# A Fourier transform over 3136 points, factored 56 by 56 where it was 64 by 49

## The chip, the cores and the metric

The kernel is one program on one core of a Trainium2 chip. The metric is device microseconds of that core from start to end of one execution; lower is better. The kernel before was timed three times: 1010.18, 1008.93 and 1010.29 us, median 1010.18 us.

## The reference

The input `x` is 8 sequences of 3136 rows of 256 numbers. The kernel computes, in single precision,

```python
X = np.fft.fft(x, axis=1)            # over the 3136 rows
X = np.fft.fft(X, axis=2)            # over the 256 columns
x = X.real.astype(np.float32)
mu = np.mean(x, axis=-1, keepdims=True)
var = np.mean((x - mu) ** 2, axis=-1, keepdims=True)
xn = (x - mu) / np.sqrt(var + 1e-06) * g_ln
ch = np.maximum(xn @ w_ch1, 0.0) @ w_ch2     # 256 -> 1024 -> 256
return x + ch
```

`g_ln`, `w_ch1` and `w_ch2` are inputs.

## The kernel before, in words

**Two halves per sequence.** The input is real and only the real part is wanted, so of the 3136 frequencies of a sequence (a batch, b = 0 to 7) only half have to be computed; a column of the kernel stands for frequency k and gives the output rows k and N-k. There are 1567 such columns in a batch and they are worked off in chunks of 256 (49 chunks, c).

**Step 1** of the transform runs over u, the 64 values with n = 49u + v. The 25 values of v that have to be kept (the others follow by symmetry) are laid out on two halves of the 128 partitions as 14 slots (`NS`), two slots to a unit (`NU` = 7, index i). For batches 1 to 7 each unit goes through a chain of small steps: `load_x` (SP's DMA queue), `fold_zw` and `fold_eo` (POOL), `fold_hi` (ACT, a rounding to the short float32 form, fp32r), `fold_lo` (POOL, the rest), `step1` (PE, three products for high and low pieces, L262, into PSUM bank `y`), a copy by ACT (L265), and `store1` to a scratch in DRAM. For batch 0 the products are full float32 (L255, L257), the folds are DVE's, and the stores go through ACT's and POOL's DMA queues in turn. `ends` and `step1_ends` treat columns 0 and 128 of the rows. A unit has two slots of 2 x 128 columns, so one product of L262 has 512 columns.

**Step 2.** `relayout` reads the scratch back with the rows turned round, as `s2` on `KP` = 112 partitions and 16 groups of 98 columns (the first has 99). `step2(m)` is one pair of groups: for each group and each of two halves h a full float32 product (L309), which PE runs as two instructions with a weight load each, so 8 instructions for a pair and 8 pairs in a batch, 64 pairs in all. For the first pair one more small product is added (L313). ACT copies the result into the chunk (`ck`, `ckh`: L332, L330) and DVE forms the low pieces (`ckl`, L334).

**The rest of the work** is the network: `moe1_a` (6 products of 256 columns, L354, and ACT and DVE work on them), `moe1_b` (L368, L369) and `moe2` (12 products of 256 columns, L404) for each of 8 parts of a chunk, and `residual` (the real output itself and its variance, 8 instructions per chunk, L428).

**Order.** The order of PE, ACT, DVE and POOL is written out by hand, and each engine works its list off in that order. A prologue (from L685) brings in batch 0, converts the weights of the network and fills PE's waiting time with products on zeros (`warm_up`, L682). Then a loop over steps s (from L825), one part of one chunk each: `moe1_b(s-1)`, `moe1_a(s)`, what `late[s]` holds, `moe2(s-3)`, what `after[s]` holds. `add` and `add_late` fill those lists. `step2(m)` stands three steps before the chunk that it begins, at the same step as the chunk's `residual`; where two pairs begin in one chunk, the second uses bank `y`. `steps1` gives the step of each unit of step 1: in 20 places over batches 2 to 7 that is the very step that holds step 2 and the residual, behind these on PE.

Of the kernel before, what the change touches and what calls it, by code (L numbers as in the profile page):

```python
# [29 lines left out]
NV = 25  # L30
# [9 lines left out]
NS = 14  # L40
ROWS = NB * N
NU = NS // 2
KP = 8 * NS


def unit_k(unit):
    if unit == 0:
        return np.concatenate([[0, N // 2], 64 * np.arange(1, 25), 32 + 64 * np.arange(24)])
    return unit + 64 * np.arange(49)


def runs():

    units = [unit for g in range(16) for unit in (g, 16 + g)]
    return [r for unit in units for r in (((49, unit),) if unit else ((24, 64), (24, 32)))]


def group_bounds():
    return [0] + [99 + 98 * g for g in range(16)]


def tables():
    u = np.arange(64)[:, None]
    t1 = np.zeros((64, 64))
    t1[:, :33] = np.cos(2 * np.pi * u * np.arange(33) / 64)
    t1[:, 33:] = np.sin(2 * np.pi * u * np.arange(1, 32) / 64)
    th = np.zeros((64, 64))
    th[:, 1:32] = -np.sin(2 * np.pi * u * np.arange(1, 32) / 64)
    th[:, 33:] = np.cos(2 * np.pi * u * np.arange(1, 32) / 64)
    tu = np.zeros((128, 388))  # L70
    for par in range(2):
        s = slice(64 * par, 64 * par + 64)
        tu[s, s] = t1
        tu[s, 128 + 64 * par:192 + 64 * par] = -t1
        tu[s, 256 + 64 * par:320 + 64 * par] = th
        tu[s, 384 + 2 * par] = 1.0
        tu[s, 385 + 2 * par] = np.cos(np.pi * np.arange(64))
    vs = ((0, np.arange(1, 15)), (1, np.append(np.arange(15, NV), 0)))
    tab = np.zeros((2, 2, 2, NS, 2, HALF))
    tz = np.zeros((4, NS, 50))  # L80
    t = 0
    for g in range(16):
        for q in range(2):
            k = unit_k(g + 16 * q)
            n = len(k)
            for par, v in vs:
# [3 lines left out]
                for comp in range(2):  # L90
                    rows = tab[par, comp, q, :m]
                    if n == 50:
                        half = np.flatnonzero(k % 64 == 32 * comp)
# [5 lines left out]
    tab = tab.transpose(3, 0, 1, 2, 4, 5).reshape(112, 2, HALF)  # L99
    tz = np.concatenate([tz.reshape(4 * NS, 50), np.zeros((KP - 4 * NS, 50))])  # L100
# [18 lines left out]
def input_rows():  # L119

    v = np.full((2, NS), -1)
    v[0] = np.arange(1, 15)
    v[1, :11] = np.append(np.arange(15, NV), 0)
    n = np.where(v[:, None] < 0, N, 49 * np.arange(64)[None, :, None] + v[:, None])
    minus = np.where(v[:, None] <= 0, N, N - n)
    both = np.stack([n, minus], 2).reshape(128, 2, NU, 2)
    return both.transpose(2, 0, 1, 3).reshape(NU, 128, 4)  # L130


def output_rows():

    k = np.concatenate([k0 + 64 * np.arange(n) for n, k0 in runs()])
# [11 lines left out]
def tile_kernel(ctx: ExitStack, tc: tile.TileContext, x, g_ln, w1, w2, tu, tab, tz, ty, tw, out):  # L147
# [14 lines left out]
    t1_hi = weights.tile([128, 128], F32R, name="t1_hi")  # L162
    t1_lo = weights.tile([128, 128], F32R, name="t1_lo")
    tu_s = const.tile([128, 388], F32, name="tu_s")
    tab_s = const.tile([KP, 2, HALF], F32, name="tab_s")
    tz_s = const.tile([KP, 50], F32, name="tz_s")
    tw_all = const.tile([128, 640], F32, name="tw_all")
# [4 lines left out]
    xs = const.tile([128, NU, 4, D], F32, name="xs")  # L172
    zmu = const.tile([KP, 2, 128], F32, name="zmu")
    masked = const.tile([128, KP], F32, name="masked")
# [4 lines left out]
    def load_x(b, i):  # L179
        in_order(nc.sync.dma_start(xs[:, i], x[b, i]))  # L180
# [3 lines left out]
    def ends(b, p0=0, p1=NS, eng=nc.gpsimd):  # L184

        if p0 == 0:
            e0c[b] = work.tile([128, NS, 2], F32, tag="e0c", name=f"e0c{b}")
        e = e0c[b]
        xp = xs[:, p0 // 2:p1 // 2, :, 0:129:128]
        eng.tensor_tensor(out=e[:, p0:p1].rearrange("p (i a) c -> p i a c", a=2), in0=xp[:, :, 0:2],  # L190
                          in1=xp[:, :, 2:4], op=ALU.add)
        if p1 < NS:
            return
        eng.tensor_tensor(out=masked[:, :4 * NS].rearrange("p (c s) -> p c s", c=4),
                          in0=e[:, None, :, 0].to_broadcast([128, 4, NS]),
                          in1=tu_s[:, 384:388, None].to_broadcast([128, 4, NS]), op=ALU.mult)

    def fold_zw(b, i, eng):

        if i > 3 and b == 0:  # L200
# [3 lines left out]
        z, w = (t[:, 256 * h:256 * h + 256].rearrange("p (s d) -> p s d", s=2) for h in range(2))  # L204
# [5 lines left out]
    def fold_eo(b, i):  # L210
        z, w = zw.pop((b, i))
        f = work.tile([128, 2, 2, 128], F32, tag="fold", name=f"f{b}_{i}")
        nc.gpsimd.tensor_tensor(out=f[:, :, 0], in0=z, in1=w, op=ALU.add)
        nc.gpsimd.tensor_tensor(out=f[:, :, 1], in0=z, in1=w, op=ALU.subtract)
        pieces[b, i] = [f]

    def fold_hi(b, i):
        hi = moving.tile([128, 2, 2, 128], F32R, tag="f_hi", name=f"fh{b}_{i}", bufs=2)
# [3 lines left out]
    def fold_lo(b, i):  # L222
        f, hi = pieces[b, i]
        lo = moving.tile([128, 2, 2, 128], F32R, tag="f_lo", name=f"fl{b}_{i}", bufs=2)
# [633 lines left out]
```

## Time and profile before

| | |
|---|---|
| times of three runs | 1010.18, 1008.93, 1010.29 us |
| profiled execution, first to last instruction | 1008.9 us |
| PE busy | 99% of the span, 8289 products |
| DVE, ACT, POOL busy | 81%, 53%, 25% |
| granted TensorE clock | 1.0 throughout |
| chain of work that ended last | PE 93%, DVE 4%, ACT 2%, DMA 1% |
| moved by DMA | 92.10 MB, mean 91 GB/s |

The span is 1.3 us under the median of the runs. Times inside it count from its start. A product is pipelined: its duration in the profile (some 280 ns) is longer than its share of PE's time, which is the distance from its start to the start of the next. The chain of work that ended last gives these distances: a row of it is a run of instructions of one line, with the time from one to the next summed up.

### The profile page before, as it was taken

What the parts mean: (1) busy time and instruction counts of PE and PEld (TensorE: products, weight loads), DVE (VectorE), ACT (ScalarE), POOL (GpSimd) and SP (SyncE); (2) the same over time, 40 slices, a digit from 0 to 9 for tenths busy, and PEclk for the clock granted to TensorE, in tenths of its full rate; (3) what the DMA queues carried; (4) which work ended last, traced back from release to release, by engine and by line L of the source; (5) the groups of instructions that cost most, each with busy time, mean ns of one, the idle gap of its engine ahead of it and who ended that gap; (6) DMA issues with size and microseconds to landing.
All of it is one profiled execution on the core that took longest, in us unless ns stands there. A gap on an engine that the chain in (4) does not pass through costs nothing.

```text
span 1008.9 us, 21765 instructions
## 1 busy us (share of the span) xinstructions
PE 998.4 (99%) x8289; PEld 976.5 (97%) x8289; DVE 817.2 (81%) x2190; ACT 534.7 (53%) x1416; POOL 248.5 (25%) x278
## 2 busy tenths in 40 slices
PE   9899999999999999999999999999999999999998
PEld 6699999999999999999999999999999999999998
DVE  6688887888778788878887888888788878887887
ACT  3555555555555555555555555554555554554553
POOL 1146533134213232312341224123323200000000
PEclk9999999999999999999999999999999999999999
DMA  9943352214221261121521242211311112100101
GB/s 343 265 164 95 116 168 74 85 53 136 85 93 55 74 177 65 56 85 60 158 84 54 84 130 91 94 54 63 116 43 43 54 55 83 41 24 22 43 22 43
DMA packets 41528, 92.10 MB, mean 91 GB/s; under 512 B 4176, under 2 KB 18704, under 8 KB 40528
## 3 DMA queue, kind: packets, MB, share of 16 engines
q1 hardware_dynamic: 40016, 88.87, 26.8%
q8 instruction: 66, 1.08, 0.5%
q0 software_dynamic: 320, 1.05, 0.3%
q10 hardware_dynamic: 1088, 0.79, 0.2%
q14 instruction: 38, 0.31, 0.1%
HBM read 50.32 MB, written 40.37 MB: 90 GB/s over the span
## 4 chain that ended last, share of the span: by engine, by line
PE 93%; DVE 4%; ACT 2%; DMA 1%; issue 0%; SPq 0%; DVEq 0%; ACTq 0%
PE acc L404 51%; PE ab L354 26%; PE ps L309 6%; PE psy L428 4%; PE ps L262 3%; DVE h_lo L369 1%; PE pw L682 1%; PE ps L255 1%; DMA scratch<-s 1%; PE ps L257 1%; DVE h L360 1%; DVE h L361 1%; ACT h_hi L368 0%; DMA s<-scratch 0%; ACT asb L359 0%
## 5 line engine op out<-in xcount | busy, mean ns | idle before, releaser
L404 PE MATMUL acc<-w_hi,h_lo 128*128 128x256 f32 x1568 | 437.9, 279 | 0.2 <-DVE h_lo L369 0.2
L404 PE MATMUL acc<-w_lo,h_hi 128*128 128x256 f32 x1568 | 437.7, 279 | 0.0
L404 PE MATMUL acc<-w_hi,h_hi 128*128 128x256 f32 x1568 | 437.6, 279 | 0.0
L368 ACT ACTIVATE h_hi<-h 128x512 fp32r<-128x512 f32 x392 | 249.3, 636 | 308.4 <-DVE h L361 308.3
L369 DVE SCALAR_TENSOR_TENSOR h_lo<-h,h_hi 128x512 fp32r<-128x512 f32 x392 | 282.0, 719 | 158.1 <-ACT h_hi L368 157.0
L404 PEld LDWEIGHTS acc<-w_hi,h_lo 128*128 128x128 f32 x1568 | 296.7, 189 | 0.6 <-DVE h_lo L369 0.4
L404 PEld LDWEIGHTS acc<-w_lo,h_hi 128*128 128x128 f32 x1568 | 295.4, 188 | 0.0
L404 PEld LDWEIGHTS acc<-w_hi,h_hi 128*128 128x128 f32 x1568 | 295.1, 188 | 0.0
L354 PE MATMUL ab<-ckl,w_hi 128*128 128x256 f32 x768 | 218.5, 285 | 1.8 <-DVE h L361 1.8
L354 PE MATMUL ab<-ckh,w_lo 128*128 128x256 f32 x768 | 214.9, 280 | 0.5 <-ACT ckh L330 0.3
L354 PE MATMUL ab<-ckh,w_hi 128*128 128x256 f32 x768 | 214.5, 279 | 0.0
L225 POOL TENSOR_TENSOR fl<-f,fh 128x512 fp32r<-128x512 f32 x49 | 64.2, 1309 | 518.6 <-ACT fh L219 512.4
L360 DVE TENSOR_TENSOR h<-asb,ab 128x256 f32<-128x256 f32 x384 | 158.2, 412 | 1.5 <-ACT asb L359 1.5
L361 DVE TENSOR_TENSOR h<-asb,ab 128x256 f32<-128x256 f32 x384 | 158.1, 412 | 0.0
L354 PEld LDWEIGHTS ab<-ckl,w_hi 128*128 128x128 f32 x768 | 145.3, 189 | 5.9 <-ACT w_hi L539 1.5
L354 PEld LDWEIGHTS ab<-ckh,w_lo 128*128 128x128 f32 x768 | 144.7, 188 | 3.1 <-ACT ckh L330 0.5
L354 PEld LDWEIGHTS ab<-ckh,w_hi 128*128 128x128 f32 x768 | 144.6, 188 | 0.0
L359 ACT COPY asb<-ab 128x256 f32<-128x256 f32 x384 | 137.8, 359 | 8.1 <-PE ab L354 6.2
L265 ACT COPY s<-ps 128x508 f32<-128x508 f32 x56 | 32.7, 584 | 64.9 <-PE ps L262 51.0
L309 PE MATMUL ps<-tab_s,s 112*128 112x98 f32 (+1 forms) x512 | 65.6, 273 | 1.5 <-DMA s<-scratch 1.5
L309 PEld LDWEIGHTS ps<-tab_s,s 112*128 112x128 f32 x512 | 61.9, 192 | 2.0 <-issue 2.0
L330 ACT CAST ckh<-ps 128x392 fp32r<-128x392 f32 (+49 forms) x112 | 39.7, 356 | 40.6 <-PE ps L309 40.4
(108 smaller groups left out, 980.5 us busy)
## 6 DMA issues: line engine op xcount, KB each, us to landing
xs<-x SPq DMA_DIRECT2D x56, 512.0 KB, 3.8
out<-o SPq DMA_DIRECT2D x96, 256.0 KB, 2.0
scratch<-s SPq DMA_DIRECT2D x49, 256.0 KB, 2.3
s<-scratch SPq DMA_DIRECT2D x7, 1792.0 KB, 9.8
w1p_all<-w SPq DMA_DIRECT2D x8, 512.0 KB, 8.3
scratch<-s POOLq DMA_DIRECT2D x4, 256.0 KB, 6.3
s<-scratch SPq DMA_DIRECT2D x2, 448.0 KB, 5.3
s<-scratch SPq DMA_DIRECT2D x1, 896.0 KB, 11.2
```

Of the source, the lines that this page charges most:

```text
L225: nc.gpsimd.tensor_tensor(out=lo, in0=f, in1=hi.bitcast(F32), op=ALU.subtract)
L265: nc.scalar.copy(s[:, :, :, :127], ps[:, :, :, :127])
L309: nc.tensor.matmul(ps[:, h, k0 - base:k1 - base], s2[b][:KP, g, 128 * h:128 * h + 128], tab_s[:, h, k0:k1], start=(h == 0 and g == 2 * j), ...
L330: nc.scalar.copy(hi, src)
L354: nc.tensor.matmul(pt, wt[wi][:, j, fs], ch[xi][:, j, :w], start=(n == 0), stop=(n == 2))
L359: nc.scalar.copy(asb[:, :w], pa)
L360: nc.vector.tensor_tensor(out=h[:, :w], in0=asb[:, :w], in1=pb, op=ALU.add)
L361: nc.vector.tensor_tensor(out=h[:, w:], in0=asb[:, :m], in1=pb[:, :m], op=ALU.subtract)
L368: nc.scalar.activation(h_hi, h, AF.Relu)
L369: nc.vector.scalar_tensor_tensor(out=h_lo, in0=h, scalar=0.0, in1=h_hi.bitcast(F32), op0=ALU.max, op1=ALU.subtract)
L404: nc.tensor.matmul(acc[c, i][:, side], hs[xi][:, h0:h0 + 128], ws[wi][:, f], start=(f == 0 and side == 0 and n == 0), stop=(f == 7 and n = ...
L428: nc.tensor.matmul(ps[:, j, :129 + j], ck[:, j], ty_s[:, j, :129 + j], start=(j == 0), stop=True, skip_group_check=True)
```

## The change

The factors become 56 and 56. Step 1 runs over 56 values of u on 112 partitions (`XP`), and 29 values of v have to be kept: 28 fill 14 slots as before, and the value v = 0 gets a fifteenth slot, on the first 56 partitions, with its own load (`x0` into `xz`) and its own short unit (i = `NU` = 7, one slot). Step 2 has 14 groups of 112 columns on 116 partitions, so 7 pairs in a batch, where it was 16 groups of 98 on 112 and 8 pairs. For batches 1 to 7 step 1's three products are made for each slot alone, 256 columns each, six for a full unit and three for the short one. The steps of the units are set anew, none of them at the step of step 2 and the residual. The last unit's store takes three slots. The table `tw_all` is put into one of the buffers of `ck_hi`; `tz_s`, `zmu` and `masked` become smaller. The core of the diff:

```diff
-NS = 14
+R1 = 56
+XP = 2 * R1
+NU = 7
+NS = 2 * NU + 1
+NG = 14
+KP = 8 * 2 * NU + 4
+KZ = 4 * NS
+NM = NG // 2
 def group_bounds():
-    return [0] + [99 + 98 * g for g in range(16)]
+    return [0] + [2 * R1 + 1 + 2 * R1 * g for g in range(NG)]
...
-    xs = const.tile([128, NU, 4, D], F32, name="xs")
+    xs = const.tile([XP, NU, 4, D], F32, name="xs")
+    xz = const.tile([XP, D], F32, name="xz")
...
     def load_x(b, i):
-        in_order(nc.sync.dma_start(xs[:, i], x[b, i]))
+        if i == NU:
+            in_order(nc.sync.dma_start(xz[:R1], x0[b]))
+        else:
+            in_order(nc.sync.dma_start(xs[:, i], x[b, i]))
...
+        eng.tensor_copy(e[:, NS - 1], xz[:, 0:129:128])
...
+    def slots(i):
+
+        return 1 if i == NU else 2
+
+    def fold_eo(b, i, eng=nc.gpsimd):
+        n = slots(i)
+        z, w = zw.pop((b, i)) if n > 1 else (xz[:, None, 1:129], xz[:, None, 255:127:-1])
+        f = work.tile([128, 2, 2, 128], F32, tag="fold", name=f"f{b}_{i}")[:XP, :n]
+        eng.tensor_tensor(out=f[:, :, 0], in0=z, in1=w, op=ALU.add)
+        eng.tensor_tensor(out=f[:, :, 1], in0=z, in1=w, op=ALU.subtract)
...
+        if b == 0 and n == 1:
+            nc.tensor.matmul(ps, tu_p, pieces.pop((b, i))[0], start=True, stop=True)
...
             p = pieces.pop((b, i))
-            for n, (ti, xi) in enumerate(PASSES):
-                nc.tensor.matmul(ps, (t1_hi, t1_lo)[ti], p[xi],
-                                 start=(n == 0), stop=(n == 2))
+            for a in range(n):
+                for j, (ti, xi) in enumerate(PASSES):
+                    nc.tensor.matmul(ps[:, a], (t1_hi, t1_lo)[ti], p[xi][:, a],
+                                     start=(a == 0 and j == 0), stop=(j == 2),
+                                     skip_group_check=True)
...
     def store1(b, i, eng=nc.sync):
-        s = s1[b][:, 2 * i:2 * i + 2]
+        n = 3 if i == NU - 1 else 2
...
-    for m in range(3, 64):
+    for m in range(3, NM * NB):
...
-    steps1 = {1: [17, 20, 23, 26, 28, 31, 34]}
-    for b in range(2, NB):
-        need = 8 * (b * REG // CW) - 3
-        steps1[b] = sorted([need - 46, need - 45] +
-                           [behind(need - d) for d in (56, 40, 32, 24, 16)])
     for b in range(1, NB):
         need = 8 * (b * REG // CW) - 3
-        at = steps1[b]
-        ends_at = need - (58 if b > 1 else 30)
+        behind = (54, 45, 38, 30, 25, 21, 14, 34)
+        at = [need - d for d in behind] if b > 1 else [17, 20, 23, 28, 30, 33, 35, 25]
+        ends_at = need - (55 if b > 1 else 30)
...
-        add(at[-1] + 2, relayout, b)
+        add(max(at) + 2, relayout, b)
...
             load_x(0, 1)
+            load_x(0, NU)
...
             ends(0, 6, 10)
             fold_zw(0, 3, nc.vector)
+            fold_eo(0, NU)
             step1(0, 3)
+            step1(0, NU)
```

## Rows read from the trace of the kernel before

**Rows 1.** The page's first part (busy time and share of the span of each engine, instructions) and the first line of its fourth (the chain that ended last).

```profile
PE 998.4 (99%) x8289; PEld 976.5 (97%) x8289; DVE 817.2 (81%) x2190; ACT 534.7 (53%) x1416; POOL 248.5 (25%) x278
...
PE 93%; DVE 4%; ACT 2%; DMA 1%; issue 0%; SPq 0%; DVEq 0%; ACTq 0%
```

**Rows 2.** Busy time in three stretches of the span; behind the length come busy us and instructions of PE, PEld, DVE, ACT and POOL, then the granted clock, the share of the DMA engines and GB/s.

```profile
8.12:22.14 14.02, 14.02 (x72) 12.29 (x71) 11.54 (x25) 5.50 (x14) 3.60 (x7) 1.00 1.03 411
22.14:34.28 12.14, 10.61 (x33) 4.45 (x32) 8.37 (x15) 6.25 (x12) 1.15 (x2) 1.00 0.77 237
...
64.00:990.00 926.00, 924.79 (x7840) 917.29 (x7840) 756.61 (x2046) 498.50 (x1329) 232.78 (x251) 1.00 0.24 79
```

**Rows 3.** The longest of PE's waits from 64 us to the end: total us, times, longest.

```profile
PE ps L262 <- DVE ckl L334: 1.2, 1, 1.2
```

**Rows 4.** The chain that ended last, from 206 to 234 us: start, us, engine, output, line, instructions.

```profile
206.22 1.41 PE acc L404 x12
207.64 0.71 PE ab L354 x6
...
218.80 0.70 PE ps L262 x3
...
220.19 1.36 PE acc L404 x12
221.55 0.68 PE ab L354 x6
...
231.75 0.87 PE ps L309 x8
232.62 0.92 PE psy L428 x8
```

**Rows 5.** One of the three like groups of L404's products, by shape, from 64 to 990 us: count, busy us, mean ns of one (the pipelined duration), idle before.

```profile
L404 PE MATMUL acc<-w_hi,h_lo 128*128 128x256 f32 x1504 | 419.9, 279 | 0.0
```

**Rows 6.** The chain that ended last, in the first six stretches of 16 to 20 us that begin with step 2 and a residual and hold no step 1 (from 844 us on), one row of each.

```profile
848.66 1.36 PE acc L404 x12
...
867.90 1.36 PE acc L404 x12
...
886.12 1.41 PE acc L404 x12
...
904.87 1.41 PE acc L404 x12
...
924.43 1.36 PE acc L404 x12
...
942.64 1.41 PE acc L404 x12
```

**Rows 7.** The same view where a unit of step 1 stands right behind the residual, the first products of L404 behind it: the first and the last of 20 such places.

```profile
136.01 1.41 PE acc L404 x12
...
827.87 1.41 PE acc L404 x12
```

**Rows 8.** The chain that ended last through the end of step 1 of batch 0.

```profile
21.24 0.43 PE ps L255 x2
...
22.14 0.59 ACT s L265
...
23.02 6.31 DMA scratch<-s
...
29.54 4.61 DMA s<-scratch
```

**Rows 9.** PE's instructions in order of time: the first of unit 4's products in batch 0, and the last filler with the start of step 2 (start, us, in brackets the idle time before and its releaser).

```profile
15.47 0.59 PE L255 MATMUL ps<-zw,tu_s 128*128 128x256 f32 x2
...
29.35 3.40 PE L682 MATMUL pw<-warm_h 128*128 128x512 bf16 x15
34.28 0.66 PE L309 MATMUL ps<-tab_s,s 112*128 112x99 f32 x4 [1.54 <-DMA s<-scratch]
```

**Rows 10.** POOL's instructions in order of time, 14 to 16 us.

```profile
14.46 1.62 POOL L269 DMA_DIRECT2D scratch<-s  x2 [3.94 <-ACT s L243]
16.11 0.23 POOL L190 TENSOR_TENSOR e0c<-xs 128x8 f32<-128x8 f32 x1
```

**Rows 11.** Groups of POOL's instructions by shape: count, busy us, mean ns of one, idle before.

```profile
L214 POOL TENSOR_TENSOR f<-zw 128x256 f32<-128x256 f32 x49 | 50.2, 1024 | 0.0
L213 POOL TENSOR_TENSOR f<-zw 128x256 f32<-128x256 f32 x49 | 39.2, 799 | 3.1
```

**Rows 12.** DMA queues: POOL's (q0) in the microsecond from 26 us, SP's (q1) in the one from 27 us, POOL's in the one from 28 us (packets, MB, share of 16 engines), and the issues of the scratch stores on POOL's queue (KB each, median us to landing).

```profile
q0 software_dynamic: 58, 0.19, 47.3%
...
q1 hardware_dynamic: 176, 0.33, 86.9%
...
q0 software_dynamic: 5, 0.02, 5.4%
...
scratch<-s POOLq DMA_DIRECT2D x4, 256.0 KB, 6.3
```

**Rows 13.** The relayout of batch 1 in the order of SP's queue and its landing (KB each, median us), and PE's first product that reads it.

```profile
130.20 0.33 SPq L276 DMA_DIRECT2D s<-scratch  x1
...
s<-scratch SPq DMA_DIRECT2D x7, 1792.0 KB, 9.8
...
152.10 0.58 PE L309 MATMUL ps<-tab_s,s 112*128 112x99 f32 x4
```

More of the change, by code (lines that the diff above doesn't have):

```diff
@@ L39 @@
 HW = 576
-NS = 14
+R1 = 56
[6 more added lines that the diff above has]
+NM = NG // 2
 ROWS = NB * N
-NU = NS // 2
-KP = 8 * NS
 def unit_k(unit):
     if unit == 0:
-        return np.concatenate([[0, N // 2], 64 * np.arange(1, 25), 32 + 64 * np.arange(24)])
-    return unit + 64 * np.arange(49)
+        return np.concatenate([[0, N // 2], R1 * np.arange(1, 28), 28 + R1 * np.arange(28)])
+    return unit + R1 * np.arange(R1)
 def runs():
-    units = [unit for g in range(16) for unit in (g, 16 + g)]
-    return [r for unit in units for r in (((49, unit),) if unit else ((24, 64), (24, 32)))]
+    units = [unit for g in range(NG) for unit in (g, NG + g)]
+    return [r for unit in units for r in (((R1, unit),) if unit else ((27, R1), (28, 28)))]
@@ new lines, in slot_rows @@
+def slot_rows():
+    v = np.full((2, NS), -1)
+    v[0] = np.append(np.arange(1, 15), 0)
+    v[1, :2 * NU] = np.arange(15, 29)
+    return v
+def tables():
+    u = np.arange(R1)[:, None]
+    k1 = np.arange(1, 28)
+    t1 = np.zeros((R1, R1))
+    t1[:, :28] = np.cos(2 * np.pi * u * np.arange(28) / R1)
+    t1[:, 28:29] = np.cos(np.pi * u)
+    t1[:, 29:] = np.sin(2 * np.pi * u * k1 / R1)
+    th = np.zeros((R1, R1))
+    th[:, 1:28] = -np.sin(2 * np.pi * u * k1 / R1)
+    th[:, 29:] = np.cos(2 * np.pi * u * k1 / R1)
+    tu = np.zeros((XP, 3 * XP + 4))
+    for par in range(2):
+        r = slice(R1 * par, R1 * par + R1)
+        for m, t in enumerate((t1, -t1, th)):
+            tu[r, XP * m + R1 * par:XP * m + R1 * par + R1] = t
+        tu[r, 3 * XP + 2 * par] = 1.0
+        tu[r, 3 * XP + 1 + 2 * par] = np.cos(np.pi * np.arange(R1))
@@ L79, in tables @@
     tab = np.zeros((2, 2, 2, NS, 2, HALF))
[L80 removed]
+    tz = np.zeros((4, NS, R1 + 1))
     t = 0
[L82 removed]
+    for g in range(NG):
         for q in range(2):
[L84 removed]
+            k = unit_k(g + NG * q)
             n = len(k)
[L86 removed]
+            for par, v in enumerate(slot_rows()):
+                v = v[v >= 0]
                 al = 2 * np.pi * ((v[:, None] * k) % N) / N
@@ L119, in input_rows @@
 def input_rows():
[L124 to L130, printed above, removed]
+    v = slot_rows()[:, None, :2 * NU]
+    n = R1 * np.arange(R1)[None, :, None] + v
+    minus = np.where(v == 28, N, N - n)
+    both = np.stack([n, minus], 2).reshape(XP, 2, NU, 2)
+    return both.transpose(2, 0, 1, 3).reshape(NU, XP, 4)
 def output_rows():
-    k = np.concatenate([k0 + 64 * np.arange(n) for n, k0 in runs()])
+    k = np.concatenate([k0 + R1 * np.arange(n) for n, k0 in runs()])
     plus = (N * np.arange(NB)[:, None] + k).ravel()
@@ L208, in fold_zw @@
         eng.tensor_tensor(out=w, in0=a[:, :, 255:127:-1], in1=c[:, :, 1:129], op=ALU.add)
[L210 to L214, printed above, removed]
+    def slots(i):
[6 more added lines that the diff above has]
+        eng.tensor_tensor(out=f[:, :, 1], in0=z, in1=w, op=ALU.subtract)
         pieces[b, i] = [f]
     def fold_hi(b, i):
-        hi = moving.tile([128, 2, 2, 128], F32R, tag="f_hi", name=f"fh{b}_{i}", bufs=2)
+        hi = moving.tile([128, 2, 2, 128], F32R, tag="f_hi", name=f"fh{b}_{i}", bufs=2)[:XP, :slots(i)]
         nc.scalar.copy(hi, pieces[b, i][0])
@@ L247, in step1 @@
     def step1(b, i):
         alloc1(b)
+        n = slots(i)
         ps = psum.tile([128, 2, 2, 128], F32, tag="y" if b else f"acc{i % 2}", name=f"ps1_{b}_{i}",
-                       bufs=1 if b else 2)
-        if b == 0:
+                       bufs=1 if b else 2)[:XP, :n]
+        if b == 0 and n == 1:
+            nc.tensor.matmul(ps, tu_p, pieces.pop((b, i))[0], start=True, stop=True)
+        elif b == 0:
             z, w = zw.pop((b, i))
-            for h in range(2):
+            for h, t in ((0, tu_p), (1, tu_n)):
@@ L765, in tile_kernel @@
             nc.sync.dma_start(tab_s[:, :, gb[8]:], tab[:, :, gb[8]:])
-            for i in range(NU):
+            for i in range(NU + 1):
                 load_x(1, i)
```

123 lines of the change are left out of this document (55 added, 68 removed).

## The prediction

> **What bounds the kernel now.** I read the busy shares first, then the chain that ended last, then the waits of PE, then the stretches of the span. PE is busy 99% of the span and makes 93% of the chain [rows 1], and from 64 us to the end nothing but 1.2 us of one wait stands out [rows 2, 3]. So between 64 and 990 us time is the sum of the distances between PE's products, and an instruction less there is time less; DVE with 757 of 926 us and POOL with 233 have room [rows 2]. Before 34 us it is another matter: step 1 of batch 0 keeps PE busy without a gap from 8.12 to 22.14 us, its last store and the relayout follow one upon the other, and step 2 starts on the landing [rows 2, 8, 9]. What is added to that path delays everything behind it.
>
> **Step 2.** Each pair is 8 instructions; 64 pairs become 56, and none of the three pairs in the prologue goes. So 64 instructions leave the loop. Eight take 0.87 us there, 0.109 us each [rows 4]. The new ones have 112 columns, not 98, a width that no row shows; the nearest are the residual's, 129 and 130 columns, full float32 too: eight take 0.92 us, 0.115 each [rows 4]. Below, 98 columns' price is the bound, since nothing makes a wider product cheaper. With 0.109 the gain is 64 x 0.109 = 7.0 us; with 0.115 it is 512 x 0.109 - 448 x 0.115 = 4.3 us. I take 7.0: 31 columns more cost 6 ns, part of which is the change back to other products, and 14 columns more should cost under 3. A check from another side: the float32 products of 256 columns take 0.215 us (two in 0.43) [rows 8], 0.84 ns a column, so 112 columns need 94 ns for themselves, still under the 109 that 98 columns take; something that doesn't go with the columns sets the distance.
>
> The Trainium skill speaks against that in "TensorE: Matmul & The Clock Gate", section "Back-to-back issue gap": it gives an isolated gap of N / 2.4 + 2.5 ns for N columns, so that time goes with columns, of which step 2 keeps as many as it had; by it the 64 instructions would return little more than 2.5 ns each, 0.2 us. The trace disagrees, 98 and 129 columns lying within 6 ns [rows 4]. What it would make of the time is the second rival.
>
> **Step 1, batches 1 to 7.** A unit is three products of 512 columns, 0.70 us [rows 4]. Six of 256 columns should be the same: 6 of L354 take 0.71 or 0.68 us, each with its own weight load [rows 4]. New is the short unit: three products more, half of 0.70, in 7 batches: +2.45 us (2.4 to 2.6). Its steps on POOL, ACT and SP are hidden: POOL is busy a quarter of the time [rows 2]. The load on SP's queue waits for the fold that reads `xz`, issued a step earlier, and holds up the stores behind it for about that. The relayout of batch 1 comes one step (2.1 us) later; now it is issued at 130.20 us, lands 9.8 us later and is read at 152.10 [rows 13], so 12 us cover it. If that cover were gone, PE would wait for what is missing.
>
> **The new steps.** The 1.2 us wait is a unit of batch 1 that wants bank `y` two steps behind a second pair [rows 3]. There the changed loop has no second pair (they fall from 14 to 6): -1.2 us. It could come back at one of three other places with that distance (0 to +1.2 us).
>
> **The prologue.** The order on POOL decides. Its two store issues run from 14.46 to 16.08 us, `ends` to 16.34 [rows 10]; then comes the short unit's `fold_eo`, two operations on 128 elements. For 256 elements such a pair takes 0.80 + 1.02 us [rows 11]; for half I estimate 1.0. The result is there at about 17.4, while PE, through with unit 3, is free at 15.47 [rows 9]: 1.9 us of waiting, then the product, 0.43 [rows 8], and 0.2 where `ends` has a copy more. Step 1 ends 2.5 us later. Not all of it reaches step 2. The last store takes 6.31 us now, because SP's queue is in its way: most of its packets go between 26 and 27 us, the rest only after SP's 0.33 MB [rows 8, 12]. Issued at 25.5 it would come behind that load and, with three slots instead of two, land at perhaps 30.3, 1.0 us later than now; the relayout with 116 rows in place of 112 takes 0.2 us more. PE's filler ends 2.5 us later, at 35.25, so the present 1.54 us of idling [rows 9] shrinks. I take +1.4 us. The bounds: -1.8, if only the product delays PE (+0.4) and the store takes 2.2 us less behind a thinner queue; +4.8, if all 2.5 us stay, the store grows with its rows (6.31 x 336/256, +2.0) and the relayout by 0.2.
>
> **PE's two paces.** The chain's rows show a thing that the sum can't pass over: twelve products of L404 take 1.41 us in some stretches and 1.36 in others, six of L354 0.71 or 0.68 [rows 4]; the duration in the profile is 281 ns in the one and 276 in the other (my reading of the stretches of rows 6), and holds until something else runs on PE. The group's mean, 419.9 us / 1504 = 279.2 ns [rows 5], puts the quick share at (281 - 279.2) / 5 = 0.36. A step is 0.08 us dearer when slow, and some 376 steps lie in the loop: 30 us between all quick and all slow. Where a unit of step 1 stands right behind the residual, all 20 stretches begin slow [rows 7]; without step 1, three of six are quick [rows 6]; and in the middle of a stretch the 512-column products turn slow to quick at 219 us [rows 4]. The change takes away all 20 such places, and its 256-column products look to PE like those around them, so I expect stretches like those of rows 6: share 0.36 to between 0.4 and 0.5, -2.0 us with 0.43. Nothing in the trace says what chooses the pace, so the bounds are wide: with shares of 0.65 and 0.2, -9 to +5 us.
>
> **Sum.** -7.0 + 2.45 - 1.2 + 1.4 - 2.0 = -6.35 us. The profiled span is 1008.9, so 1002.5; the median of the runs lies 1.3 above that span, so 1003.8 us. The forecast's own range, with the pace's bounds and the smaller ones beside them, is 996 to 1010.
>
> **Rivals.** First, on the other side: the pace turns slow nearly everywhere. The place is the exit from each block of step 2 and residual; 112-column products and one-slot units could leave PE in the slow pace as the old units did. With a share of 0 the price is 0.36 x 30 = 10.8 in place of the -2.0: 1003.8 + 12.8 = 1016.6. It decides from a share below 0.21, where 0.15 x 30 = 4.4 us eat up the other terms (7.0 - 2.45 + 1.2 - 1.4). For it: rows 7. Against: rows 6. Chance 0.09. Second: step 2 goes by columns. Then 112 columns cost 0.109 x 112/98 = 0.124 us, 448 of them what 512 cost now, and the sum loses 7.0: 1010.8. Against it stand the residual's rows; 0.04. Third: the prologue takes its upper bound, 3.4 us more, because PE's wait reaches step 2 in full: 1007.2; for it speaks that POOL's four stores all take some 6.3 us [rows 12]; 0.12. Fourth: the pace turns quick for most of the loop, a share of 0.8, since the short weight loads and absent 512-column products leave it alone: 1003.8 - 0.37 x 30 = 992.7; 0.10. Fifth: the loop doesn't do what the change says, because the new steps bring the 1.2 us wait at bank `y` [rows 3] into each of 7 batches: 1003.8 + 8.4 = 1012.2; against it, no unit stands nearer than two steps behind a second pair; 0.03. The forecast keeps 0.62.
>
> **How the numbers follow.** A measurement of this kernel can tell about 0.2%, 2.0 us, so faster means below 1008.2 and slower above 1012.2. Of the forecast's 0.62, 0.55 fall below and 0.07 between; of the first rival 0.08 above and 0.01 between; the second's 0.04 between; of the third 0.08 below and 0.04 between; the fourth's 0.10 below; of the fifth 0.02 above and 0.01 between. So faster 0.73, same 0.17, slower 0.10. The range leaves out about 0.1 on each side, at the fourth rival below and at the first and fifth above: 996 to 1011.5.
>
> **What would show it.** L309 with 448 instructions and eight in 0.87 to 0.90 us of the chain; L262's successor with 315 products, a full unit in 0.68 to 0.71; no wait of a unit for `ckl`; in the prologue PE waiting for POOL's fold between units 3 and 4, and step 2 starting at 35.5 to 36 us; mean duration of L404 near 278.8 ns. I am wrong if L309's eight take 1.0, if step 2 starts after 37.5, or if that mean leaves 277.8 to 280.

## The result, and the profile after

The changed kernel takes 1019.86 us (median of four runs, 1014.21 to 1020.98); the kernel before, in four runs beside it, 1009.8 us. The ratio is 1.0089 (95% interval 1.0068 to 1.0111): 0.9% slower, where 1003.8 us were forecast, and outside the range of 996 to 1011.5. The profiled execution took 1020.98 us; its span is 1019.2 us, where that of the kernel before is 1008.9.

The page's busy line, the clock granted in 40 slices of the span (a digit is tenths of full speed, 9 stands for 90% or more, and the kernel before has a 9 in all 40) and the chain that ended last, by engine, of the changed kernel:

```profile
PE 991.6 (97%) x8394; PEld 973.3 (95%) x8395; DVE 813.9 (80%) x2182; ACT 538.5 (53%) x1415; POOL 261.1 (26%) x309
...
PEclk9899998999999999999999999999999999999999
...
PE 84%; DMA 9%; DVE 4%; issue 1%; ACT 1%; POOL 1%; SPq 0%; POOLq 0%; DVEq 0%; ACTq 0%
```

PE has fewer busy microseconds than before and still ends later: its share fell from 99% to 97%, DMA's share of the chain rose from 1% to 9% [rows 1], and the clock, at full speed throughout before, falls in some slices. The longest waits of PE (total us, times, longest) name the DMA:

```profile
PE ps L338 <- DMA s<-scratch: 13.8, 2, 7.7
PE ps L279 <- POOL f L240: 2.2, 1, 2.2
PE ab L383 <- DVE ckl L363: 2.0, 1, 2.0
PE psy L457 <- DMA ty_s<-ty: 1.3, 1, 1.3
```

`s<-scratch` is the relayout, L338 step 2 (L309 before); L290 is step 1 (L262), L433 the twelve `acc` products (L404), L383 `ab` (L354), L457 the residual (L428). Line numbers move from kernel to kernel, the tiles' names stay. The chain shows both places, first the prologue, then batch 1 (start, us, what):

```profile
25.90 0.59 ACT s L293
26.50 0.29 issue
26.78 6.57 DMA scratch<-s
...
33.54 8.93 DMA s<-scratch
42.48 0.14 issue
42.61 1.17 PE ps L338 x4
...
122.68 0.72 PE ps L290 x6
...
124.09 1.36 PE acc L433 x12
125.45 0.88 PE ps L338 x8
126.33 0.91 PE psy L457 x8
...
146.27 26.78 DMA s<-scratch
173.05 0.04 issue
173.09 1.19 PE ps L338 x4
```

The relayout of batch 0 is made in three parts; the first, which step 2 waits for, takes 8.93 us where it took 4.61 [rows 8], and step 2 of batch 0 starts at 42.61, not 34.28 [rows 9]. Batch 1's relayout needs 26.78 us from issue to landing where the like took 9.8 [rows 13], and PE stands still for 7.67 us. The rows from 122.68 to 126.33 are the other side: 1.36 us for twelve products of L433, the quicker of the two values of [rows 4], and eight instructions of step 2 in 0.88, though they are 14 columns wider now.

Stretches of the changed kernel (us, then busy us and instructions of PE, PEld, DVE, ACT and POOL, the granted clock, the share of 16 DMA engines, GB/s):

```profile
42.60:52.80 10.20, 9.88 (x47) 9.13 (x47) 3.83 (x9) 3.62 (x10) 1.28 (x1) 0.58 0.43 142
88.00:94.00 6.00, 5.29 (x32) 5.32 (x33) 5.30 (x11) 3.27 (x11) 5.92 (x8) 0.72 0.51 156
165.20:173.10 7.90, 0.23 (x4) 0.04 (x2) 1.25 (x3) 0.13 (x1) 3.17 (x4) 0.85 0.24 80
173.10:182.60 9.50, 9.50 (x49) 9.20 (x50) 2.04 (x6) 4.34 (x14) 0.00 (x0) 0.59 0.04 14
182.60:990.00 807.40, 807.40 (x7077) 806.18 (x7076) 666.09 (x1814) 443.38 (x1171) 200.41 (x229) 1.00 0.22 73
```

While PE waits for nothing but the relayout (third row), the DMA engines are 24% busy, which is some 4 of 16, and move 80 GB/s. Behind three waits of PE, of 6.1 us (at 42.61), 2.0 (for `ckl`, at 88.71) and 7.7 (at 173.09), the granted clock stands at the lower of its two levels for a while. The means 0.58, 0.72 and 0.59 give an estimate of 0.42 x 10.2 + 0.28 x 6.0 + 0.41 x 9.5 = 9.9 us of full-speed time lost. The last row shows that PE waits for nothing later: from 182.6 to 990 us it is busy to the last hundredth.

The start of each batch's step 2 (its small product L313 or L342 in PE's timeline) cuts the span into pieces; "120 rows" is the first experiment below:

```
us                       before    after   120 rows
start to batch 0           34.8     43.7       38.0
batch 0 to batch 1        117.7    130.5      117.3
batch 1 to batch 2        118.9    119.8      116.7
batches 2 to 6            592.0    581.9      581.7
batch 7 to PE's end       141.9    139.8      139.8
```

So the change wins 12.2 us from batch 2 on and loses 22.6 before that. From batch 1 to batch 2 PE waits for nothing; the 3.1 us that the changed kernel takes more there than the one with 120 rows are the price of the lower clock behind the wait of 7.7 us.

### The profile page after: what moved, and what is told of

It is laid out like the page before. It is cut to its first block, busy times and chain, and to the rows that moved or that the text cites. A ratio compares the mean times of both kernels' runs of the same rounds, so it can differ in the third digit from the quotient of the medians.

```text
span 1019.2 us, 22039 instructions
## 1 busy us (share of the span) xinstructions
PE 991.6 (97%) x8394; PEld 973.3 (95%) x8395; DVE 813.9 (80%) x2182; ACT 538.5 (53%) x1415; POOL 261.1 (26%) x309
## 4 chain that ended last, share of the span: by engine, by line
PE 84%; DMA 9%; DVE 4%; issue 1%; ACT 1%; POOL 1%; SPq 0%; POOLq 0%; DVEq 0%; ACTq 0%
PE acc L433 47%; PE ab L383 24%; PE ps L338 5%; PE psy L457 4%; PE ps L290 4%; DMA s<-scratch 4%; DMA xs<-x 3%; DMA ty_s<-ty 2%; DVE h_lo L398 1%; DMA scratch<-s 1%; DVE h L389 1%; DVE h L390 1%; ACT h_hi L397 1%; PE ps L342 0%; DVE st L479 0%
## 5 line engine op out<-in xcount | busy, mean ns | idle before, releaser
L433 PE MATMUL acc<-w_hi,h_lo 128*128 128x256 f32 x1568 | 434.0, 277 | 0.4 <-DVE o L520 0.3
L433 PE MATMUL acc<-w_lo,h_hi 128*128 128x256 f32 x1568 | 433.7, 277 | 0.3 <-POOL w_lo L569 0.3
L433 PE MATMUL acc<-w_hi,h_hi 128*128 128x256 f32 x1568 | 433.7, 277 | 0.0
L398 DVE SCALAR_TENSOR_TENSOR h_lo<-h,h_hi 128x512 fp32r<-128x512 f32 x392 | 287.6, 734 | 159.1 <-ACT h_hi L397 153.7
L433 PEld LDWEIGHTS acc<-w_hi,h_lo 128*128 128x128 f32 x1568 | 295.1, 188 | 0.8 <-DVE o L520 0.5
L433 PEld LDWEIGHTS acc<-w_lo,h_hi 128*128 128x128 f32 x1568 | 295.2, 188 | 0.5 <-POOL w_lo L569 0.5
L433 PEld LDWEIGHTS acc<-w_hi,h_hi 128*128 128x128 f32 x1568 | 294.9, 188 | 0.0
L383 PE MATMUL ab<-ckl,w_hi 128*128 128x256 f32 x768 | 220.0, 287 | 2.0 <-DVE ckl L363 2.0
L383 PE MATMUL ab<-ckh,w_lo 128*128 128x256 f32 x768 | 214.3, 279 | 0.8 <-ACT w_lo L620 0.5
L383 PE MATMUL ab<-ckh,w_hi 128*128 128x256 f32 x768 | 213.4, 278 | 0.0
L251 POOL TENSOR_TENSOR fl<-f,fh 112x512 fp32r<-112x512 f32 (+1 forms) x56 | 69.3, 1238 | 497.9 <-ACT fh L245 497.9
L383 PEld LDWEIGHTS ab<-ckl,w_hi 128*128 128x128 f32 x768 | 145.4, 189 | 2.4 <-issue 2.0
L383 PEld LDWEIGHTS ab<-ckh,w_lo 128*128 128x128 f32 x768 | 145.7, 190 | 1.5 <-ACT w_lo L620 0.7
L383 PEld LDWEIGHTS ab<-ckh,w_hi 128*128 128x128 f32 x768 | 145.4, 189 | 0.0
L293 ACT COPY s<-ps 112x508 f32<-112x508 f32 (+1 forms) x64 | 35.7, 558 | 79.7 <-PE ps L290 62.5
L338 PE MATMUL ps<-tab_s,s 116*128 116x112 f32 (+1 forms) x448 | 63.1, 286 | 13.8 <-DMA s<-scratch 13.8
L338 PEld LDWEIGHTS ps<-tab_s,s 116*128 116x128 f32 x448 | 57.8, 201 | 15.0 <-DMA s<-scratch 7.9
L359 ACT CAST ckh<-ps 128x448 fp32r<-128x448 f32 (+49 forms) x104 | 38.3, 371 | 55.9 <-PE ps L338 55.9
```

Of the source, the lines that this page charges most:

```text
L251: nc.gpsimd.tensor_tensor(out=lo, in0=f, in1=hi.bitcast(F32), op=ALU.subtract)
L338: nc.tensor.matmul(ps[:, h, k0 - base:k1 - base], s2[b][:KP, g, 128 * h:128 * h + 128], tab_s[:, h, k0:k1], start=(h == 0 and g == 2 * j), ...
L359: nc.scalar.copy(hi, src)
L383: nc.tensor.matmul(pt, wt[wi][:, j, fs], ch[xi][:, j, :w], start=(n == 0), stop=(n == 2))
L398: nc.vector.scalar_tensor_tensor(out=h_lo, in0=h, scalar=0.0, in1=h_hi.bitcast(F32), op0=ALU.max, op1=ALU.subtract)
L433: nc.tensor.matmul(acc[c, i][:, side], hs[xi][:, h0:h0 + 128], ws[wi][:, f], start=(f == 0 and side == 0 and n == 0), stop=(f == 7 and n = ...
```

## The experiments

**Theory A:** 116 = 4 x 29 rows are dealt out to 4 of the 16 DMA engines, 112 rows to 16; that makes the relayout late, and the waits and the lower clock follow. **Rival B:** the relayout is late because of its place in the queue and of what moves beside it. For the loop, **theory P:** the 256-column products of step 1 keep PE at its quick pace; **rival Q:** it is the new place of the units, away from the residual.

**120 rows.**

```diff
-KP = 8 * 2 * NU + 4
+KP = 8 * NS
```

> The changed kernel with one constant altered: the contraction of step 2 has 120 rows in place of 116 (four more rows of zeros in the table, four more rows in each relayout). Theory A, the row count: 116 = 4 x 29 rows are dealt out to 4 of the 16 DMA engines, 120 = 8 x 15 rows to 15 of them. Then batch 1's relayout lands 10 to 12 us after its issue in place of 26.8 although it moves 3% more bytes, the DMA share stands at 0.9 or more while it runs in place of 0.24 to 0.44, step 2 of batch 0 starts at 35 to 37.5 us in place of 42.6, PE's waits for s<-scratch go from 13.8 us to 1.5 to 3, the granted clock shows no stretch at 0.50, and the time is 988 to 998 us, below both kernels. Theory B, the order of the queue and the traffic beside it (the x loads of the next batch, the wider stores): the relayout still lands more than 20 us after its issue and the time stays at 1014 to 1021.

998.88 us (998.74 to 999.2), ratio 0.9889 (0.9875 to 0.9904). With 3% more bytes the relayout is nearly as quick as in the kernel before (5.00 us for its first part against 4.61). Chain, one stretch and the waits of PE:

```profile
32.24 5.00 DMA s<-scratch
37.24 0.14 issue
37.38 0.67 PE ps L338 x4
```

```profile
135.70:147.00 11.30, 11.30 (x101) 11.26 (x100) 8.16 (x25) 6.45 (x20) 0.00 (x0) 1.00 0.91 223
```

```profile
PE ab L383 <- DVE h L390: 2.4, 6, 0.7
PE ps L279 <- POOL f L240: 2.1, 1, 2.1
...
PE ps L338 <- DMA s<-scratch: 1.3, 1, 1.3
```

The DMA share over the relayout is 0.91 (0.24 for it alone in the changed kernel), the clock 1.0 throughout, and the four first products of step 2 take 0.67 us, not 1.17. A holds, B falls. The forecast of the time missed by 0.9 us on the high side.

**112 and 4 rows** (shortened).

```diff
+for r0, r1 in ((0, 112), (112, KP)):
-    dma_start(s2[b][:KP, g0:g1] ..., sv[:KP, g0 * D:g1 * D])
+    dma_start(s2[b][r0:r1, g0:g1] ..., sv[r0:r1, g0 * D:g1 * D])
```

and the same for the three loads of `tab_s`.

> The changed kernel with every DMA of 116 rows (the relayouts and the three loads of step 2's table) made as two, of 112 and of 4 rows; nothing else altered. Theory A (row count): as with 120 rows, batch 1's relayout lands 10 to 12 us after its issue, the clock stays at 1.00, the time is 988 to 998 us, within 2 us of the kernel with 120 rows. Theory B (queue and traffic): two DMAs more per relayout change nothing or make it later, time 1014 to 1022.

997.34 us, ratio 0.9884 (0.9855 to 0.9914), four runs: 1002.73, 996.83, 997.85, 996.3. The profiled one is the 1002.73; in it step 2 of batch 0 waited 2.7 us and the clock fell behind that:

```profile
39.00:50.50 11.50, 11.18 (x54) 10.43 (x55) 4.71 (x11) 4.20 (x11) 1.28 (x1) 0.58 1.05 260
```

0.42 x 11.5 = 4.8 us by the same estimate; that run lies 5 to 6 us above the other three, of which there is no profile.

**92 and 20 rows in the kernel before**: the relayout's 112 rows as two DMAs, same bytes. The scratch is also named as one run of 112 rows there, where it was 14 times 8; the kernel with 112 and 4 rows has that form too, and is quick.

> The kernel before with each relayout of 112 rows made as two DMAs of 92 = 4 x 23 and 20 = 2 x 10 rows; same bytes, same order, nothing else altered. Theory A (row count): the 92 rows go through 4 engines, so batch 1's relayout lands 22 to 28 us after its issue in place of 9.8, beyond the 21.9 us until PE reads it: PE waits 1 to 5 us there, step 2 of batch 0 starts 4 to 9 us later than 34.28, and the time is 1015 to 1028 us. Theory B: the count of rows means nothing, the landing stays at 9.6 to 11 us and the time at 1009 to 1012.

1020.8 us, ratio 1.0107 (1.009 to 1.0124). Dealing out the rows otherwise slows the old kernel as much as the whole change did. The way differs from what was expected. Step 2 of batch 0 starts at 33.4 us, no later; but PE waits 7.3 us for `ty_s`, whose load stands behind the last part of that relayout in SP's queue, and the clock is at 0.51 over the 5 us behind that wait. Batch 1's relayout, issued at 137.55, lands 22 us later (expected 22 to 28), and as all stands 8 us later by then, PE waits only 0.46 us:

```profile
PE psy L429 <- DMA ty_s<-ty: 7.3, 1, 7.3
```

```profile
160.12 0.66 PE L310 MATMUL ps<-tab_s,s 112*128 112x99 f32 x4 [0.46 <-DMA s<-scratch]
```

**Other row counts**, off the path, in the kernel with 120 rows: `cut = {2: 119, 3: 117, 4: 114, 5: 110, 6: 104, 7: 96}.get(b, KP)`, with the rest as a second DMA.

> The kernel with 120 rows, with the relayouts of batches 2 to 7 made as two DMAs each: 119 + 1, 117 + 3, 114 + 6, 110 + 10, 104 + 16 and 96 + 24 rows (batch 1 stays one of 120). It asks for the rule from rows to engines. Theory A (the largest divisor of the row count that is 16 or less): 119 rows go to 7 engines, 117 to 13, 114 to 6, 110 to 11, 104 to 13, 96 to 16, so that the packets of the relayout keep about 6 to 7.5 engines busy for 119 + 1 and 6 to 7.5 for 114 + 6 and 11 to 14 for the others, and last 12 to 18 us for 119 and 114 against 7.5 to 11 us for the others. Rival A2 (only counts that are multiples of 8 or 16 are spread widely): 117 and 110 are slow as well, 18 us or more.

998.95 us (one run). From the packet records of the traces (packets of 14336 and 16384 bytes: first to last in us, the sum of their durations over that time as engines busy, and the number of packets that were under way at once for the largest part of that time):

```
rows of the DMAs   largest divisor to 16   us            engines busy   at once   kernel, batches
112                16                       7.6 to 9.1    12.6 to 14.4   16        before, 1 to 7
116                4                       18.9 to 25.3    3.4 to 3.7    4         after, 1 to 7
120                15                       9.0 to 9.9    12.5 to 13.8   15        120 rows, 1 to 7
112 + 4            16, 4                    7.3 to 8.6    11.4 to 13.6   16        112 and 4, 1 to 7
92 + 20            4, 10                   18.8 to 21.1    4.4 to 4.7    4         before with 92 and 20, 1 to 7
119 + 1            7, 1                    15.8            6.2           7         cuts, 2
117 + 3            13, 3                    8.7           10.0           13        cuts, 3
114 + 6            6, 6                    12.7            5.8           6         cuts, 4
110 + 10           11, 10                  11.3           10.5           11        cuts, 5
104 + 16           13, 16                  11.2           11.9           13        cuts, 6
96 + 24            16, 12                   8.6           13.0           16        cuts, 7
```

The number at once is the largest divisor of the main part in every row. 117 and 110 rows are not slow, so rival A2 falls; their engines busy lie a little under the 11 to 14 expected, and 110 and 104 rows last a little longer than the 7.5 to 11 us expected. The Trainium skill states this rule in "DMA: Bandwidth & Descriptors", section "Why a DMA increments its semaphore by 16 and not by 1": a DMA runs on the largest number of engines up to 16 that divides the slowest dimension of both sides. The table agrees.

**256 columns in the kernel before**, steps unchanged (shortened).

```diff
-for n, (ti, xi) in enumerate(PASSES):
-    matmul(ps, (t1_hi, t1_lo)[ti], p[xi], ...)
+for a in range(2):
+    for n, (ti, xi) in enumerate(PASSES):
+        matmul(ps[:, a], (t1_hi, t1_lo)[ti], p[xi][:, a], ...)
```

> The kernel before with the products of step 1's units cut from 512 to 256 columns and nothing else (same steps, same 112 rows). Theory P (the 256-column products keep PE at the quick pace): the first product after a unit takes 1.36 to 1.37 us in place of 1.41, the mean of the acc products falls from 279 to 277 ns, and the time is 992 to 997 us. Theory Q (the pace is set by where units stand, away from the residual): units right behind the residual are still followed by slow stretches, the quick share stays at 0.3 to 0.5, time 1006 to 1012.

1008.07 us, ratio 0.9982 (0.9973 to 0.9992): P's time is missed, Q's met. Behind its units the pace is kept all the same, as the table further down counts.

**512 columns in the kernel with 120 rows**: the reverse edit.

> The kernel with 120 rows, with the products of step 1's whole units (six per unit, 256 columns) put back to three of 512 columns; steps as they are. It asks what keeps nearly every stretch of acc products at the quick pace (113.3 ns a product; 118 slow). Theory P (the 512-column unit changes the pace): after a unit the pace is the other one, as in the kernel before, the mean of the acc products rises from 277 to 278.5 ns or more, the quick share falls to 0.4 to 0.7, time 1004 to 1012 us. Theory Q (units away from the residual, and 112-column products of step 2): the stretches stay quick, time 997 to 1001 us.

1015.92 us, ratio to before 1.0053 (1.0036 to 1.0071), 17 us above the kernel with 120 rows. The time lies beyond P's forecast. Chain:

```profile
183.25 1.36 PE acc L431 x12
184.61 0.70 PE ps L289 x3
...
186.02 1.41 PE acc L431 x12
...
192.38 1.42 PE acc L431 x12
193.79 0.36 PE ps L289 x3
...
194.85 1.36 PE acc L431 x12
```

The 512-column unit turns the pace slow (23 of 23), and the short unit (0.36 us, 256 columns) quick again (6 of 6). P's words "the pace is the other one" don't hold: behind a slow stretch the 512-column unit leaves it slow here (18 of 18), where in the kernel before it turned it quick (14 of 14).

**Units behind the residual, with 120 rows**: `behind = (54, 46, 40, 32, 45, 24, 16, 35)`, two steps later where two pairs stand.

> The kernel with 120 rows, with four of a batch's seven units of step 1 put at the steps of a residual (two steps later where two step 2s stand there), as in the kernel before; products of 256 columns as in the changed kernel. Theory P (256-column products keep the pace that was there): stretches stay quick, time 998 to 1001 us. Theory Q (what stands right behind a residual turns slow): about half of the stretches turn slow, time 1003 to 1010 us.

1002.42 us, ratio 0.9923 (0.9908 to 0.9937). Nearly all stretches stay quick (share 0.97), so Q falls here, though the time lies between the two forecasts. Of the 4.3 us between the two profiled spans, 2.4 are waits for DVE's `h` (4.8 in place of 2.4) and 1.1 a later step 2 of batch 0: behind PE's wait of 2.05 us for POOL the clock fell, to a mean of 0.66 from 17.5 to 27.5 us.

**256 columns and the new steps in the kernel before**: `steps1[b] = [need - d for d in (54, 45, 38, 30, 25, 21, 14)]` on top of the 256-column products.

> The kernel before (98 columns a group in step 2) with both other parts of the changed loop: step 1's products of 256 columns, and the units of batches 2 to 7 at the steps need - 54, 45, 38, 30, 25, 21, 14, none right behind a residual. Theory R (the 98-column products of step 2 leave the pace to either value, 256-column products only keep it): the quick share stays at 0.4 to 0.7, acc mean 278 to 279 ns, time 1003 to 1010 us. Theory Q (placement and 256 columns together suffice): quick share 0.9 or more, acc mean 277 ns or less, time 992 to 998 us.

1006.34 us, ratio 0.9965 (0.9952 to 0.9978), acc mean 279 ns: the two together don't suffice either, and Q falls. Where the pace changes is plain in the chain:

```profile
169.95 1.36 PE acc L406 x12
171.31 0.87 PE ps L311 x8
172.18 0.92 PE psy L430 x8
...
173.81 1.41 PE acc L406 x12
...
177.34 0.71 PE ps L263 x6
...
178.75 1.41 PE acc L406 x12
```

Step 2 with the residual turned it, the unit of 256 columns did not. Counted over all such places from batch 1 on (stretch ahead to stretch behind, by the distance of the starts of L404's products and their successors; quick below 115.3 ns):

```
                              unit of step 1              step 2 with residual    quick share
before                        quick>slow 8 of 8           quick>slow 8 of 12         0.40
                              slow>quick 14 of 14         slow>quick 9 of 15
256 columns in before         quick>slow 0 of 16          quick>slow 8 of 14         0.49
the same, units moved         quick>slow 0 of 17          quick>slow 15 of 21        0.49
120 rows                      quick>slow 0 of 37          quick>slow 1 of 43         0.97
120 rows, 512 columns         quick>slow 23 of 23         quick>slow 1 of 14         0.36
```

Both parts of the change are needed: in these kernels no 256-column unit turns quick into slow, and the new step 2 with the residual hardly ever does, where the old one did 15 times of 21 with the units moved. Three more runs ask what in step 2 does it.

**98 + 14 columns** for each product of step 2, 120 rows; **14 columns more** per product, into columns that nothing reads, in the kernel before with 256 columns and moved units; **18 columns more** in the kernel with 120 rows.

> The kernel with 120 rows, with each product of step 2 (112 columns) made as two, of 98 and of 14 columns; everything else as it is. The products it adds cost time of their own (about 10 to 25 us), so the mean of the acc products tells. Theory R (98-column products unsettle the pace): the acc mean rises from 276 to 278 ns or more. Rival: it stays at 276 to 277.

> The kernel before with 256-column products and moved units (before_256_moved), and behind each product of step 2 one more with the same stationary over 14 of its columns, into columns of the PSUM tile that nothing reads: 98 + 14 = 112 columns stream for each group, as in the changed kernel. Theory C (the number of columns that step 2 streams decides whether the pace survives it): the stretches stay quick, acc mean 276 to 277 ns. Theory N (it does not): the acc mean stays at 279. The added products cost 30 to 45 us of their own in either case.

> The kernel with 120 rows, with one more product of 18 columns behind each of step 2's, into columns that nothing reads: 130 columns for each group. Theory C: the pace no longer survives step 2 with the residual behind it and the acc mean rises to 278 or more. Theory N: it stays at 276. The added products cost 30 to 50 us of their own in either case.

1045.71, 1062.16 and 1048.76 us. The acc means are 276, 279 and 277 ns:

```profile
L435 PE MATMUL acc<-w_hi,h_hi 128*128 128x256 f32 x1568 | 433.2, 276 | 0.0
```

```profile
L409 PE MATMUL acc<-w_hi,h_hi 128*128 128x256 f32 x1568 | 437.0, 279 | 0.0
```

Neither the width of a product nor the sum of the columns decides; theories R and C fall. The first run's products cost more than expected (47 us over the kernel with 120 rows, not 10 to 25), and so do the second's (56 over its parent, not 30 to 45). PE's timeline tells why: from batch 1 to batch 7 an instruction of step 2 takes 108 ns in the mean in all three runs, 14 and 18 columns among them, and 110 in the kernel before. Step 2 goes by its number of instructions, as the prediction had it.

**The residual one step later**, in the kernel before with 256 columns and moved units.

> The kernel before with 256-column products and moved units (before_256_moved), and each residual one step later than now, so that a stretch of acc products stands between step 2 and the residual (steps 8c + 6, as it is for the first two chunks). If the pace changes at step 2: the stretch right behind step 2 differs from the one ahead of it. If it changes at the residual (129 and 130 columns): the stretch behind step 2 has the pace of the one ahead, and the next one, behind the residual, differs. Time 1003 to 1010 us unless the changes fall out otherwise.

1014.05 us, ratio 1.0039 (1.0023 to 1.0056), 8 us over its parent although its acc mean is 277 ns: PE waits 12.6 us for DVE's `h` in it. Here the old step 2 turns quick stretches slow, and the residual alone turns them quick again:

```profile
847.64 1.36 PE acc L406 x12
849.00 0.87 PE ps L311 x8
...
850.60 1.41 PE acc L406 x12
852.01 0.89 PE psy L430 x8
...
853.60 1.36 PE acc L406 x12
```

Counted as above, step 2 turned 17 of 34 quick stretches slow (6 of the 17 with a wait of PE behind it), the residual none of 24, and of 19 slow ones it turned 17 quick. Three units of 256 columns turned quick into slow in this run, each behind a wait of PE for `ckl`.

Why the old step 2 can turn PE slow, also with the residual right behind it, and the new one hardly ever does, stays open; the number of rows (112 against 116 and 120) was not tried by itself.

**More filler in the changed kernel**: `warm_up(41, warm_h)` in place of 15.

> The changed kernel, 116 rows, with 41 filler products in place of 15 ahead of step 2 of batch 0, so that PE is busy until about 42 us, when the late relayout lands. It prices the clock alone: if the half clock after the idle time costs what its length says (7 us and more at 0.50 behind that idle stretch), the clock stays at 1.00 there and the time falls by 3 to 5 us to 1015 to 1017. Rival: what follows waits for DMAs anyway (w2, the table's last part), and the time stays at 1018 to 1021.

1016.61 us, scattered from 1010.62 to 1022.66: not settled. In the profile the clock holds at the first place and step 2 starts at 41.99 us, but PE then waits 4.5 us for `ty_s` (1.3 in the changed kernel), and the clock falls behind that, and again behind the wait of 4.8 us for batch 1's relayout. The price of the clock alone rests on the stretches above.

**The short unit's fold on DVE**, 120 rows: `fold_eo(0, NU, nc.vector)`.

> The kernel with 120 rows, with the fold of batch 0's short unit (two additions) on DVE in place of POOL. Theory A: PE's wait of 2.1 us for POOL between units 3 and 4 goes, step 1 ends about 2 us sooner, and step 2 of batch 0 starts 1 to 2 us sooner than 37.4: time 996.5 to 998.5 us. Rival: units 4 to 6 wait for their x loads (slower with 112 rows) or the relayout is bound by its queue, and nothing is won: 998.5 to 1000 us.

997.69 us, ratio 0.9879 (0.9865 to 0.9894): PE's 2.1 us wait is gone and step 2 starts 0.65 us sooner: the last store is issued 1.7 us sooner and takes 1.1 us longer (6.88 against 5.74). The interval overlaps that of the kernel with 120 rows.

```profile
36.73 0.67 PE L338 MATMUL ps<-tab_s,s 120*128 120x113 f32 x4 [0.91 <-DMA s<-scratch]
```

**And the copy of the short slot's ends sooner.**

> The kernel with 120 rows and the fold of batch 0's short unit on DVE, with one more step: the copy of the short slot's two end columns (1.0 us on POOL, between two pieces of the ends) goes ahead, to the first piece of the ends, where POOL is idle. Theory A: PE's wait of 0.8 us for POOL's copy goes and step 2 of batch 0 starts 0.5 to 1 us sooner than 36.73: time 996.3 to 997.7 us. Rival: the store of unit 5 or the relayout's queue is bound elsewhere and it stays at 997.5 to 998.5.

997.62 us, ratio 0.988 (0.9864 to 0.9897): nothing more. The time fits both forecasts; step 2 starts at 36.81, no sooner, and still waits 1.79 us for the relayout, so the rival was right. These last two, with the kernels of 120 and of 112 and 4 rows, beat the kernel before by 11 to 12 us.

## Why the prediction was wrong, point by point

**The step that failed** is the relayout's, twice. In the prologue, "the relayout with 116 rows in place of 112 takes 0.2 us more": the first part, which step 2 waits for, took 4.3 us more (8.93 against 4.61). In the loop, the 9.8 us of [rows 13] were taken over for batch 1 and "12 us cover it"; the landing took 26.8 us and the cover was gone, with the wait that the text named for that case and gave no price. Both priced rows by their number and not by how they are dealt out. That cost, against the kernel with 120 rows: 3.9 us at the start of step 2 (8.93 against 5.00; the start is 5.2 later, the rest being a last store 0.8 us longer and an end of step 1 0.5 later), 7.7 at batch 1, and most of the 9.9 us of lower clock, which no term had. The medians differ by 21 us (1019.86 - 998.88).

**Prologue without that.** With 120 rows step 2 starts at 37.38, 3.1 us later than before: +1.4 was low, within -1.8 to +4.8. Step 1 ended 3.3 us later (forecast 2.5), with the wait for POOL's fold in it (2.1 us; forecast 1.9). The last store took 5.74 us, where 4.8 were reckoned (25.5 to 30.3), and landed 2.7 us later than before, not 1.0. Of the wait only 0.65 us reached step 2, as the run with the fold on DVE shows; this rests on one trace of each, and traces of four kernels with the prologue of 120 rows have the start between 37.38 and 38.50.

**Step 2 and step 1.** Per batch, from PE's timeline over batches 2 to 6 (distances between starts):

```
us per batch      before   120 rows
acc (L404)        66.90     65.31
ab (L354)         33.82     33.59
step 2 (L309)      7.03      6.34
small product      0.18      0.36
step 1 (L262)      5.00      5.30
residual (L428)    5.03      4.96
```

Eight instructions of step 2 take 0.88 us, as forecast, and the gain is 8 x 0.69 = 5.5 us, or 4.1 with the small product, which doubled and had no term; -7.0 was too much, the bound of -4.3 about right. The formula of the Trainium skill in "TensorE: Matmul & The Clock Gate", section "Back-to-back issue gap", given there for an isolated product, would have had step 2 return 0.2 us; these rows don't bear it out. Step 1's units cost +0.30 x 8 = 2.4 us; forecast 2.45. The 1.2 us wait for `ckl` ahead of a unit is gone; the 2.0 us one in the changed kernel stands at L383, in the late start, and not in the kernel with 120 rows.

**The pace** was mis-sized: -2.0 us with a share of 0.43. It rose to 0.97, the fourth rival's case and beyond its 0.8, and gave 8 x (1.59 + 0.23) = 14.6 us. The mean duration of L404's successor went from 279 ns [rows 5] to 276:

```profile
L433 PE MATMUL acc<-w_hi,h_lo 128*128 128x256 f32 x1568 | 433.4, 276 | 0.4 <-DVE o L520 0.3
```

The reason given, that the change takes away the 20 places behind the residual, was not the one: with units put back there the share stays 0.97. The other reason, that the new products look to PE like those around them, holds for the units (0 of 37 against 8 of 8). The scale of 30 us between all slow and all quick was too large: the share rose by 0.57 (from 0.40 by this count), and 14.6 / 0.57 gives 26.

**The sum** with measured terms for the kernel of 120 rows: -4.1 + 2.4 - 1.2 + 3.1 - 14.6 = -14.4; measured -11.0. Part of the rest is in the table of stretches: batch 0's gave 0.5 us, not the 2 of the later ones. The remainder was not taken apart. That this kernel lands within the forecast's range is in part luck: step 2 and the prologue gave less than forecast, and the pace seven times as much.

## What to carry to other kernels

Before a change alters the outer count of a DMA, factor the new count: 116 rows on 4 engines took more than twice as long as 120 rows on 15, and the four rows of zeros that make the difference cost nothing that these runs can tell. Price a transfer's cover with its landing under the new shape, and count the lower clock behind a wait as a cost of its own. A change whose sum fails at one place can still hold most of its gain: look at the stretches that nothing disturbs before giving it up.

## What the runs showed of the hardware that was not expected

- A DMA of 116 rows kept 3.4 to 3.7 DMA engines busy, one of 120 rows 12.5 to 13.8, of 119 (with 1) 6.2, of 114 (with 6) 5.8.
- Behind waits of PE of 2.0, 2.5, 2.7, 4.5, 4.8, 6.1, 7.3 and 7.7 us the granted clock fell to its lower level, behind waits of 0.9 to 1.8 us ahead of step 2 of batch 0 it did not, unless narrow products were added to it. The length of the wait alone doesn't tell: behind the wait of 1.6 to 2.2 us ahead of the short unit's product in the prologue it fell in three of the traces with that wait (the units behind the residual, the 98 + 14 columns, the 18 columns more) and not in the others, the changed kernel and the one with 120 rows among them. In the kernel with 14 columns more it fell with no wait of PE over 0.4 us, behind blocks of step 2 with the narrow products (0.50 from 36.4 to 43.1 us and from 224.1 to 227.4).
- PE has two steady distances between 256-column products, 113.3 and 117.7 ns at the same clock. All 31 512-column units that followed a quick stretch left PE slow (8 + 23), none of 70 units of 256 columns did (16 + 17 + 37) in the kernels of the table; putting 512 columns back into the quick kernel cost 17 us.
- An instruction of a float32 product of 112 columns costs what one of 98 does (eight in 0.88 and 0.87 us), and one of 14 or 18 columns put beside them nearly as much (108 ns in the mean of both kinds); the small one of 57 columns takes 178 ns where that of 50 took 91.
